# Feed-forward as block products: w_out decoded during the attention, y's operands in the experts' slots, wo's loads at group 26, five operand buffers in turn

## The chip, the cores and the metric

One NeuronCore of a Trainium2 chip runs the program. The metric is the device time of one execution in microseconds (us), the median of the runs shown. TensorE is called PE here, VectorE DVE, ScalarE ACT, GpSimd POOL and SyncE SP. SP issues all of this kernel's transfers, one after the other; DVE, ACT, PE, POOL and SP each work through their own list in order, and wait for each other by semaphores.

## What is computed

Three steps stand one behind the other; all arrays are float32 in the reference.

```python
def phi(x):                       # attention with 128 random features, 4 batches x 8 heads x 576 x 64
    h = np.einsum('bhsd,md->bhsm', x, omega) - np.sum(x * x, axis=-1, keepdims=True) / 2.0
    return np.exp(h - np.max(h, axis=-1, keepdims=True)) / np.sqrt(m)
kv = np.einsum('bhsm,bhsd->bhmd', k_p, v)
num = np.einsum('bhsm,bhmd->bhsd', q_p, kv)      # divided by q_p . sum of k_p: x, 2304 tokens x 512

for e in range(E):                # 8 experts, each token goes to the one with the largest logit
    he = np.maximum(x[mask] @ w1[e], 0.0)        # 512 -> 1024 -> 512
    out[mask] = gate_w[mask, None] * (he @ w2[e])

h = x @ w_in                      # the feed-forward: 512 -> 2048 -> 512 for all 2304 tokens
g = h * (1.0 / (1.0 + np.exp(-1.702 * h)))
return (g @ w_out).astype(np.float32)
```

## The kernel before

**Precision.** Every product is made of three matmuls. An operand x is split in two: hi is x rounded by an ACT copy to the type fp32r, lo is x - hi by a subtraction (on DVE, for some weights on POOL); hi x hi, hi x lo and lo x hi are added up in PSUM. Wherever a split is named below, it is one ACT instruction and one subtraction behind it (line 785).

**Attention and experts, merged.** The attention (a generator, line 741) and the experts (`moe_gen`, line 660) run merged by a ratio of work until the attention ends; then the experts go on alone. An expert pass b takes the 576 tokens of batch b in two halves of 288; a half does 8 products xh, xl x w into h1h, h1l (12 matmuls each) and then the second layer into the y tiles, which go to `y_dram`. Weights come through staging tiles st and are split into the slots wh0 to wh7 and wl0 to wl7 of the pool `moe`, which also holds xh, xl, h1h, h1l and y.

**The feed-forward as block products.** Both factors use a scheme with 7 products where a 2 x 2 block product has 8; the operands are sums and differences of blocks, made by `mix` (four additions into the last places of a tile z). The raw weights arrive as 64-bit words and are decoded by DVE with three integer operations per tile `raw` (`decode`, line 758).
- `prep_in(j)` (line 805): two raws of w_in, decode, mix on POOL, split into wih, wil (pool `ring`, two of each).
- `prep_out(j)` (line 821): two raws of w_out, decode, mix on POOL, two stores into `wo_dram` (768 and 128 KB). Eight of them, j = 0 to 7.
- `prep_y(b)` (line 838): two halves kp of the features of batch b; loads of z from `y_dram`, mix (POOL for kp 0, DVE for kp 1), split into yc.
- `first(j, b)` (line 974): 32 groups, the "quads", of 7 products x 6 matmuls of 128x288; ACT and DVE take the sums out of PSUM (s1, u2, u3, h), ACT applies the gate function, and two stores go to `g_dram`.
- `second(k)` (line 1072): 9 blocks of 256 tokens, 7 products x 24 matmuls of 128x256; the left operands are sums of quarters of gt, split into gs; the right ones are wo, loaded from `wo_dram` and split (`prep_w`, line 1040).

**What sets the order.** The list `jobs` holds the prep generators; `work()` advances the first of them by one step each time it is called, once per step of the experts or of a group. Before the change the list gets six `prep_out` when the attention ends (line 927), and w_in 0 and 1, y0 and the last two `prep_out` when all but one of the experts are through (line 936); y1 to y3 are put in only after the experts (line 948), when the pool `moe` has been given up for `rp`. The program's final order on each engine then comes from the compiler's scheduler.

**Buffers.** z has two buffers, raw three, gs three slots in turn: one tile of `l2` and two tags of `ring` (line 1083, two buffers each). gt (line 1052) is one tile of 256 tokens, loaded by two transfers with runs of 512 B, so a tile is free again when its last reader is through.

## Time and profile before

| what | value |
|---|---|
| median of 3 runs | 838.25 us (834.89 to 841.78) |
| the profiled execution | 839.54 us, its span 837.7 us |
| mean granted clock of TensorE in it | 0.959 |
| PE busy | 763.2 us (91%), 5922 matmuls |
| DVE busy | 517.7 us (62%) |
| ACT busy | 353.6 us (42%) |
| POOL busy | 204.8 us (24%) |
| moved by DMA | 126.64 MB, mean 151 GB/s |

The span runs from the first to the last instruction of the profiled execution. Busy time is the time in which an engine has an instruction under way; PE's matmuls are pipelined, so a busy PE can still do fewer matmuls than it could, and the count beside the busy time says how many. The attention ends at about 320 us, the experts at about 420, the first factor at about 625 with its last groups, and the second runs to the end. "A <- B" in a list of waits means that A stood still until B had ended.

### The profile page before, as it was taken

What the parts mean: (1) busy time and instruction counts of PE and PEld (TensorE: products, weight loads), DVE (VectorE), ACT (ScalarE), POOL (GpSimd) and SP (SyncE); (2) the same over time, 40 slices, a digit from 0 to 9 for tenths busy, and PEclk for the clock granted to TensorE, in tenths of its full rate; (3) what the DMA queues carried; (4) which work ended last, traced back from release to release, by engine and by line L of the source; (5) the groups of instructions that cost most, each with busy time, mean ns of one, the idle gap of its engine ahead of it and who ended that gap; (6) DMA issues with size and microseconds to landing.
All of it is one profiled execution on the core that took longest, in us unless ns stands there. A gap on an engine that the chain in (4) does not pass through costs nothing.

```text
span 837.7 us, 15256 instructions
## 1 busy us (share of the span) xinstructions
PE 763.2 (91%) x5922; PEld 735.0 (88%) x5922; DVE 517.7 (62%) x1130; ACT 353.6 (42%) x687; POOL 204.8 (24%) x158
## 2 busy tenths in 40 slices
PE   7997999999999998999747999999964999899996
PEld 6876999989999997999737999999964999899896
DVE  5877675768752625986826754423475676567653
ACT  5554653445233323223324655555663333333231
POOL 3455495165004400454332431100000000000000
PEclk9999899999999999999967999999995999999999
DMA  5556945467223306996572653344593545554411
GB/s 157 132 143 137 280 109 154 110 195 157 54 82 109 99 27 193 326 321 216 173 226 87 221 193 139 115 150 164 179 355 102 127 126 126 126 127 126 126 26 29
DMA packets 158319, 126.64 MB, mean 151 GB/s; under 512 B 63904, under 2 KB 139680, under 8 KB 157344
## 3 DMA queue, kind: packets, MB, share of 16 engines
q1 hardware_dynamic: 158240, 125.59, 51.1%
q8 instruction: 48, 0.79, 0.4%
q14 instruction: 31, 0.25, 0.1%
HBM read 78.69 MB, written 40.39 MB: 142 GB/s over the span
## 4 chain that ended last, share of the span: by engine, by line
PE 62%; DMA 14%; DVE 11%; ACT 4%; issue 3%; POOL 3%; SPq 2%; POOLq 0%; ACTq 0%; DVEq 0%
PE m_ps L110 18%; PE pa L983 10%; DMA gt<-g_dram 6%; PE qa L1095 5%; PE pc L983 5%; PE qm L1095 4%; PE w_ps L110 3%; DVE gs L787 3%; PE num L414 3%; PE pb L983 3%; PE kv_ps L372 2%; PE pb L1095 2%; DMA z<-wo_dram 2%; PE tq L400 1%; PE pr L314 1%
## 5 line engine op out<-in xcount | busy, mean ns | idle before, releaser
L983 PE MATMUL pa<-yc,wih 128*128 128x288 f32 x512 | 112.3, 307 | 19.8 <-ACT yc L786 12.7
L983 PEld LDWEIGHTS pa<-yc,wih 128*128 128x128 f32 x512 | 86.4, 196 | 23.3 <-ACT yc L786 14.1
L110 PE MATMUL m_ps<-xh,wh 128*128 128x288 f32 x256 | 78.9, 308 | 4.9 <-DVE h1l L678 4.9
L1095 PE MATMUL qa<-wo,gs 128*128 128x256 f32 x648 | 82.6, 283 | 0.4 <-ACT gs L786 0.4
L1095 PEld LDWEIGHTS qa<-wo,gs 128*128 128x128 f32 x648 | 79.7, 190 | 1.0 <-ACT gs L786 0.9
L645 POOL TENSOR_TENSOR wl<-st,wh 128x1024 fp32r<-128x1024 f32 x23 | 54.5, 2375 | 94.8 <-ACT wh L643 94.7
L983 PE MATMUL pa<-yc,wil 128*128 128x288 f32 x256 | 77.5, 303 | 0.0
L110 PE MATMUL m_ps<-xh,wl 128*128 128x288 f32 x256 | 76.6, 299 | 0.0
L110 PE MATMUL m_ps<-xl,wh 128*128 128x288 f32 x256 | 76.5, 299 | 0.0
L999 DVE TENSOR_TENSOR h<-pc,u 128x288 f32<-128x288 f32 x64 | 28.1, 454 | 68.4 <-PE pc L983 55.3
L786 ACT ACTIVATE gs<-gt 128x1024 fp32r<-128x1024 f32 x36 | 38.1, 1059 | 71.8 <-PE qm L1095 45.7
L783 POOL TENSOR_TENSOR z<-z 128x256 f32<-128x256 f32 (+1 forms) x48 | 43.2, 920 | 99.4 <-DVE z L767 78.2
L1095 PE MATMUL qm<-wo,gs 128*128 128x256 f32 x432 | 58.8, 292 | 8.6 <-DVE gs L787 7.5
L1095 PEld LDWEIGHTS qm<-wo,gs 128*128 128x128 f32 x432 | 55.6, 198 | 10.3 <-DVE gs L787 8.7
L329 DVE TENSOR_REDUCE small<-pr 128x4 f32<-128x512 f32 (+1 forms) x80 | 51.1, 639 | 13.7 <-PE pr L321 6.3
L678 DVE SCALAR_TENSOR_TENSOR h1l<-m_ps,h1h 128x288 fp32r<-128x288 f32 x64 | 28.9, 453 | 46.4 <-ACT h1h L675 46.2
L643 ACT ACTIVATE wh<-st 128x1024 fp32r<-128x1024 f32 (+1 forms) x33 | 33.9, 1033 | 54.3 <-DMA st<-in_moe_w_dram 23.9
L1000 ACT ACTIVATE g<-h 128x288 f32<-128x288 f32 x96 | 40.2, 439 | 36.2 <-DVE h L999 31.4
L787 DVE TENSOR_TENSOR gs<-gt,gs 128x1024 fp32r<-128x1024 f32 x36 | 44.0, 1222 | 18.1 <-ACT gs L786 18.0
L983 PE MATMUL pc<-yc,wih 128*128 128x288 f32 x256 | 54.4, 297 | 0.1
L110 PEld LDWEIGHTS m_ps<-xh,wh 128*128 128x128 f32 x256 | 48.7, 190 | 5.9 <-DVE h1l L678 5.3
L675 ACT ACTIVATE h1h<-m_ps 128x288 fp32r<-128x288 f32 x64 | 25.7, 405 | 59.1 <-PE m_ps L110 58.8
(175 smaller groups left out, 2039.3 us busy)
## 6 DMA issues: line engine op xcount, KB each, us to landing
g_dram<-g SPq DMA_DIRECT2D x64, 288.0 KB, 2.5
gt<-g_dram SPq DMA_DIRECT2D x16, 1024.0 KB, 9.0
st<-in_moe_w_dram SPq DMA_DIRECT2D x31, 512.0 KB, 5.3
raw<-in_moe_w_out_dram SPq DMA_DIRECT2D x16, 512.0 KB, 6.0
raw<-in_moe_w_in_dram SPq DMA_DIRECT2D x16, 512.0 KB, 4.9
z<-wo_dram SPq DMA_DIRECT2D x7, 1024.0 KB, 6.7
wo_dram<-z SPq DMA_DIRECT2D x8, 768.0 KB, 5.3
y_dram<-y SPq DMA_DIRECT2D x32, 144.0 KB, 3.6
```

The lines of the kernel that those rows point to most:

```text
L110: ins = nc.tensor.matmul(out=ps, lhsT=a, rhs=b, start=start and n == 0, stop=stop and n == 2)
L329: nc.vector.tensor_reduce(out=pm, in_=ps[:, :w], axis=AX.X, op=ALU.max, negate=on_act)
L643: nc.scalar.activation(out=hi[:, :, s], in_=st[:, :, s], func=ACTF.Copy)
L645: eng.tensor_tensor(out=lo[:, :, s], in0=st[:, :, s], in1=f32(hi)[:, :, s], op=ALU.subtract)
L678: nc.vector.scalar_tensor_tensor(out=hl[:, f], in0=ps, scalar=0.0, in1=f32(hh[:, f]), op0=ALU.max, op1=ALU.subtract)
L783: eng.tensor_tensor(out=z[:, o], in0=z[:, a], in1=z[:, b], op=op)
L786: nc.scalar.activation(out=hi, in_=src, func=ACTF.Copy)
L787: eng.tensor_tensor(out=lo, in0=src, in1=f32(hi), op=ALU.subtract)
L983: nc.tensor.matmul(out=ps, lhsT=w[:, a, kp], rhs=x[:, kp, y], start=start and kp + m == 0, stop=kp == 1 and m == 2, skip_group_check=True,)
L999: nc.vector.tensor_tensor(out=h, in0=ps, in1=add, op=ALU.add)
L1000: nc.scalar.activation(out=dst, in_=h, func=ACTF.Gelu_apprx_sigmoid)
L1095: nc.tensor.matmul(out=ps, lhsT=x[:, f], rhs=w[i][:, f], start=start and f + m == 0, stop=f == NP - 1 and m == 2, skip_group_check=True,)
```

## The change

It touches five things.
1. **w_out's eight jobs** run in a pool `early` of their own, from the 200th step of the merged loop on, one step of a job every third step. The pool has one z and two raw buffers, and before each raw load ACT writes one element of the raw tile from the last h1h result (`mark`), so that the load can't start ahead of that expert's work.
2. **y's operands** get homes in slots that are there already: y0 in the pool `r0`, made as soon as the attention ends; y1 in w0 to w3, y2 in xh, xl, w4 and w5, made during the last expert when the slots are given up (`chunks`); y3 in w6, w7, h1h and h1l, made after it. The halves hi and lo of a weight become one tile w0 to w7 for it. The pools `rp` and `l2` go.
3. **The order of the last eight groups** is by b, and wo's loads come by the table `after`: wo0 and gt 0 behind group 25 (the 26th), wo1 and wo2 behind group 27, wo3 and wo4 behind 29, the last two behind the first step of block 0.
4. **gt** is loaded in two tiles, one for each half of the features, with runs of 1 KB.
5. **The operands gs** take five places in turn (two tags of `ring` and the two z buffers, and one tile of `l1`) where there were three.

```diff
+    EARLY = 200
+    early = tc.alloc_tile_pool(name="early", bufs=1, side="right")
...
-        hi = moe.tile(shape, F32R, tag=f"wh{c}", name=f"wh{c}")
-        lo = moe.tile(shape, F32R, tag=f"wl{c}", name=f"wl{c}")
+        w = moe.tile([P, 2] + shape[1:], F32R, tag=f"w{c}", name=f"w{c}")
+        hi, lo = w[:, 0], w[:, 1]
...
                 nc.scalar.activation(out=hh[:, f], in_=ps, func=ACTF.Relu)
+                mark[0] = f32(hh[0:1, f, 0:1])
...
-        raw = pool.tile([P, DM], I64, tag="raw", name="raw", bufs=3)
+        raw = pool.tile([P, DM], I64, tag="raw", name="raw", bufs=2)
+        if pool is early:
+            nc.scalar.activation(out=raw.bitcast(F32)[0:1, 0:1], in_=mark[0], func=ACTF.Copy)
...
-        return pool.tile(shape, F32, tag="z", name="z", bufs=2)
+        return pool.tile(shape, F32, tag="z", name="z", bufs=1 if pool is early else 2)
...
+    def prep_y(zpool, b, homes, chunks):
         for kp in range(2):
+            while prep["free"] < 2 * NW * (B - 1) + chunks[kp]:
+                yield "wait"
+            hi, lo = (slot(*homes[2 * kp + i], [P, 7, HS], f"y{'hl'[i]}") for i in range(2))
...
+        early_jobs = [prep_out(early, j) for j in range(NP)]
...
             tick()
+            if clock[0] >= EARLY and clock[0] % 3 == 0:
+                work(early_jobs)
         att_done[0] = True
...
-        r0 = None
-        jobs += [prep_out(fw, j) for j in range(6)]
+        r0 = tc.alloc_tile_pool(name="r0", bufs=1)
+        homes = [[(r0, f"r{i}") for i in range(4)]]
+        homes += [[(moe, f"w{i}") for i in range(4)]]
+        homes += [[(moe, "xh"), (moe, "xl"), (moe, "w4"), (moe, "w5")]]
+        homes += [[(moe, "w6"), (moe, "w7"), (moe, "h1h"), (moe, "h1l")]]
+        jobs.append(prep_y(fw, 0, homes[0], (0, 0)))
...
-                jobs += [prep_in(fw, ring, 0), prep_in(fw, ring, 1), prep_y(fw, 0, y0), prep_out(fw, 6), prep_out(fw, 7)]
-            work()
+                jobs += [prep_in(fw, ring, 0), prep_in(fw, ring, 1)]
+                jobs += [prep_y(fw, 1, homes[1], (NW, NW)), prep_y(fw, 2, homes[2], (NW, NW + 2))]
+            work(early_jobs)
+            work(jobs, 2 if x_done[0] == B else 1)
...
-        quads += [(6, 0), (6, 1), (7, 0), (7, 1), (6, 2), (7, 2), (6, 3), (7, 3)]
+        quads += [(j, b) for b in range(B) for j in (NP - 2, NP - 1)]
...
+            parts = [pool.tile([P, NP, 2 * P], F32, tag=tg, name="gt", bufs=1) for pool, tg in g_homes[k % 2]]
...
+        GS = ((ring, "wh", 2), (ring, "wl", 2), (fw, "z", 2), (fw, "z", 2), (l1, "gs", 1))
...
-                pool, tg, n = ((l2, "gs", 1), (ring, "wh", 2), (ring, "wl", 2))[operands[0] % 3]
+                pool, tg, n = (l1, "gs", 1)
+                if operands[0]:
+                    pool, tg, n = GS[(operands[0] - 1) % len(GS)]
...
+        after = {
+            25: [lambda: prep_w(0), lambda: gts.update({0: load_g(0)})],
+            27: [lambda: prep_w(1), lambda: prep_w(2)],
+            29: [lambda: prep_w(3), lambda: prep_w(4)],
+        }
...
-            if n == 28:
-                prep_w(0)
-                gts[0] = load_g(0)
-                prep_w(1)
-            if n in (29, 30, 31):
-                prep_w(n - 27)
```

In the rows below, a number behind a name tells tiles of one name apart, and what stands in brackets is what the instruction waits for.

**DVE just behind the attention's last step (the copy tot_i).** Before, the decode of the first w_out job (z<-raw) stands there, between two h1l splits of the expert pass b = 2.

```order
L678 SCALAR_TENSOR_TENSOR h1l_4364<-m_ps_4409,h1h_4363 128x288 [waits Activation_49]
L911 CAST tot_i_3906<-small_116 128x1 [waits PE_49]
L760 TENSOR_SCALAR z_3946<-raw_3928 128x512 [waits DMAHW4_49,DMAHW5_49,DMAHW3_49,DMAHW6_49,SP_sequencer_49,DVE_49]
L764 SCALAR_TENSOR_TENSOR z_3946<-raw_3928,z_3946 128x512 [waits DVE_49]
L760 TENSOR_SCALAR z_3946<-raw_3930 128x512 [waits DMAHW7_49]
L767 SCALAR_TENSOR_TENSOR z_3946<-raw_3928,z_3946 128x512 [waits DVE_49]
L764 SCALAR_TENSOR_TENSOR z_3946<-raw_3930,z_3946 128x512 [waits DVE_49]
L645 TENSOR_TENSOR wl1_4442<-st_4161,wh1_4441 128x1024 [waits DMAHW5_49,PE_49,Activation_49]
L678 SCALAR_TENSOR_TENSOR h1l_4364<-m_ps_4426,h1h_4363 128x288 [waits Activation_49]
L760 TENSOR_SCALAR z_4019<-raw_4001 128x512 [waits DMAHW0_49]
```

After, two more h1l splits are done ahead of the block, and the place is taken by the mix of y0's second half (z_4239<-z_4239), the two lo halves of y0 (yl), two operations of w_in's decode (z_4607) and a weight split:

```order
L651 TENSOR_TENSOR w1_4495<-st_4267,w1_4495 128x1024 [waits DMAHW5_49,PE_49,Activation_49]
L686 SCALAR_TENSOR_TENSOR h1l_4425<-m_ps_4498,h1h_4424 128x288 [waits Activation_49]
L791 TENSOR_TENSOR z_4239<-z_4239 128x288 [waits DMAHW2_49,DMAHW3_49,DMAHW1_49,DMAHW4_49,SP_sequencer_49,DVE_49]
L941 CAST tot_i_4034<-small_119 128x1 [waits PE_49]
L791 TENSOR_TENSOR z_4239<-z_4239 128x288 [waits DMAHW3_49]
L791 TENSOR_TENSOR z_4239<-z_4239 128x288 [waits DVE_49] x2
L795 TENSOR_TENSOR yl_4168<-z_4169,yh_4167 128x2016 [waits DMAHW7_49,DMAHW0_49,Activation_49]
L795 TENSOR_TENSOR yl_4238<-z_4239,yh_4237 128x2016 [waits Activation_49]
L768 TENSOR_SCALAR z_4607<-raw_4587 128x512 [waits DMAHW6_49,DMAHW5_49,DVE_49]
L768 TENSOR_SCALAR z_4607<-raw_4589 128x512 [waits DMAHW6_49]
L651 TENSOR_TENSOR w2_4530<-st_4478,w2_4530 128x1024 [waits DMAHW4_49,Activation_49]
L686 SCALAR_TENSOR_TENSOR h1l_4425<-m_ps_4515,h1h_4424 128x288 [waits Activation_49]
```

The decode of w_out has left the place; the h1l split that follows now stands behind y0's whole chain.

**ACT where the experts end and the first groups begin.** Before, the splits of y1, y2 and y3 (yc2, yc4, yc6) stand among the evacuations of the first groups (s1, u2 from PSUM, g through the gate function):

```order
L1000 ACTIVATE g_5309<-h_5390 128x288 [waits DVE_49]
L786 ACTIVATE yc2_5231<-z_5248 128x2016 [waits DMAHW4_49,DMAHW3_49,Pool_49]
L786 ACTIVATE yc2_5231<-z_5276 128x2016 [waits DMAHW5_49,DMAHW4_49,DVE_49]
L786 ACTIVATE yc4_5233<-z_5304 128x2016 [waits DMAHW0_49,DMAHW7_49,Activation_49,Pool_49]
L990 ACTIVATE s1_5406<-pa_5399 128x288 [waits PE_49,Activation_49]
L990 ACTIVATE s1_5494<-pa_5487 128x288 [waits PE_49,Activation_49]
L1000 ACTIVATE g_5397<-h_5417 128x288 [waits DVE_49]
L1000 ACTIVATE g_5308<-h_5452 128x288 [waits DVE_49]
L990 ACTIVATE u2_5442<-pa_5399 128x288 [waits PE_49]
L786 ACTIVATE yc4_5233<-z_5343 128x2016 [waits DMAHW3_49,DMAHW2_49,DVE_49]
```

After, only y3 (yh_5272) stands behind the experts' last h1h (h1h_5019); y2's second half (yh_4927) comes before the first s1:

```order
L682 ACTIVATE h1h_5019<-m_ps_5130 128x288
L794 ACTIVATE yh_4927<-z_4929 128x2016 [waits DMAHW2_49,DMAHW3_49,DVE_49,PE_49]
L1012 ACTIVATE s1_5270<-pa_5263 128x288 [waits PE_49]
L1012 ACTIVATE s1_5341<-pa_5334 128x288 [waits PE_49]
L1012 ACTIVATE u2_5300<-pa_5263 128x288 [waits PE_49]
L1012 ACTIVATE u2_5378<-pa_5334 128x288 [waits PE_49]
L1022 ACTIVATE g_5261<-h_5285 128x288 [waits DVE_49]
L1012 ACTIVATE s1_5425<-pa_5418 128x288 [waits Activation_49]
L1012 ACTIVATE u3_5327<-pa_5263 128x288 [waits PE_49]
L1012 ACTIVATE u3_5411<-pa_5334 128x288 [waits PE_49]
L794 ACTIVATE yh_5272<-z_5274 128x2016 [waits DMAHW4_49,DMAHW2_49,Pool_49]
L1022 ACTIVATE g_5262<-h_5329 128x288 [waits DVE_49]
```

The splits of y1 and y2 moved ahead, in among the h1h of the last expert.

**ACT where the first factor ends.** Before, the splits of wo5 and wo6 follow the last g, and the operands of the first block (gs) follow them:

```order
L786 ACTIVATE wo4_7433<-z_7431 128x2048 [waits DMAHW2_49]
L1000 ACTIVATE g_7436<-h_7526 128x288 [waits DVE_49]
L786 ACTIVATE wo5_7532<-z_7530 128x2048 [waits DMAHW4_49,PE_49]
L786 ACTIVATE wo6wh_7540<-z_7538 128x2048 [waits DMAHW2_49]
L786 ACTIVATE gs_7603<-gt_7218 128x1024 [waits PE_49,Activation_49]
L786 ACTIVATE gs_7544<-s1_7506 128x1024
```

After, the same two splits, wo6 first, stand ahead of the last g and of the operand gs_7540, which the third product of block 0 reads:

```order
L1022 ACTIVATE g_7431<-pa_7432 128x288 [waits DMAHW1_49,PE_49]
L1022 ACTIVATE g_7431<-h_7492 128x288 [waits DVE_49]
L794 ACTIVATE wo6wh_7536<-z_7534 128x2048 [waits DMAHW5_49,PE_49]
L794 ACTIVATE wo5h1h_7526<-z_7524 128x2048 [waits DMAHW3_49,PE_49]
L1022 ACTIVATE g_7430<-h_7520 128x288 [waits DVE_49]
L794 ACTIVATE gs_7540<-s1_7500 128x1024
L794 ACTIVATE gs_7571<-s1_7500 128x1024 [waits DVE_49,Activation_49]
```

The order between the last wo splits and that operand is the same; two of the earlier wo splits (wo3, wo4) are further ahead than they were.

## Rows read from the trace of the kernel before

**Rows 1.** 40-us windows: busy (count) of PE, PEld, DVE, ACT, POOL; clock; DMA; GB/s.

```profile
200.00:240.00 40.00, 40.00 (x358) 37.92 (x357) 27.20 (x98) 13.33 (x33) 2.38 (x1) 1.00 0.29 70
240.00:280.00 40.00, 40.00 (x329) 39.14 (x328) 17.29 (x58) 13.54 (x24) 10.96 (x5) 1.00 0.37 113
280.00:320.00 40.00, 40.00 (x314) 38.38 (x314) 18.54 (x79) 12.42 (x29) 8.02 (x4) 1.00 0.19 61
...
400.00:440.00 40.00, 23.64 (x136) 21.08 (x134) 21.90 (x34) 12.38 (x18) 16.56 (x16) 0.80 0.64 201
440.00:480.00 40.00, 34.87 (x222) 33.86 (x223) 28.27 (x44) 21.11 (x43) 13.27 (x12) 0.86 0.48 157
480.00:520.00 40.00, 40.00 (x303) 40.00 (x302) 21.25 (x40) 22.07 (x53) 9.56 (x12) 1.00 0.50 170
...
600.00:640.00 40.00, 21.97 (x158) 20.57 (x157) 24.25 (x24) 21.46 (x33) 0.00 (x0) 0.81 0.91 298
```

**Rows 2.** Waits of PE in 300:400: engine, line, releaser: us, times, longest.

```profile
PE m_ps L110 <- DVE h1l L678: 4.9, 2, 4.0
```

**Rows 3.** Chain of waits in 315:346: start, us, what.

```profile
325.25 4.80 DMA raw<-in_moe_w_out_dram
...
330.17 0.44 DVE z L760
...
334.64 0.38 DVE h1l L678
```

**Rows 4.** Waits of PE in 400:480.

```profile
PE pa L983 <- ACT yc L786: 12.7, 5, 6.0
```

**Rows 5.** Chain of waits in 398:456.

```profile
419.00 8.00 DMA wo_dram<-z
...
428.85 3.74 DMA z<-y_dram
...
432.75 4.35 POOL z L783 x3
...
438.00 1.90 ACT yc L786
439.92 2.27 DVE yc L787
```

**Rows 6.** Chain of waits in 590:646.

```profile
629.12 6.67 DMA z<-wo_dram
...
635.81 1.92 ACT wo6wh L786
...
637.75 2.29 DVE wo6wl L787
...
641.24 4.83 PE pb L1095 x22
```

**Rows 7.** Waits of PE in 645:840.

```profile
PE qm L1095 <- DVE gs L787: 7.5, 5, 2.3
```

**Rows 8.** Waits of DVE in 640:838.

```profile
DVE s L1077 <- DMA gt<-g_dram: 20.8, 5, 5.6
```

**Rows 9.** DVE by line in 320:480: shapes, count; busy, mean ns; idle before, releasers.

```profile
L764 DVE SCALAR_TENSOR_TENSOR z<-raw,z 128x512 int32<-128x512 int32 x24 | 19.0, 797 | 0.3
...
L767 DVE SCALAR_TENSOR_TENSOR z<-raw,z 128x512 int32<-128x512 int32 x24 | 17.2, 725 | 0.2
L760 DVE TENSOR_SCALAR z<-raw 128x512 int32<-128x512 int32 x26 | 14.3, 561 | 6.7 <-DMA raw<-in_moe_w_out_dram 4.6 <-DMA wo_dram<-z 1.5 <-DMA raw<-in_moe_w_in_dram 0.3
```

**Rows 10.** POOL by line in 320:480.

```profile
L831 POOL TENSOR_TENSOR z<-z 128x256 f32<-128x256 f32 x32 | 30.5, 973 | 76.0 <-DMA raw<-in_moe_w_out_dram 40.9 <-DVE z L767 32.7 <-ACT g L1000 2.3
```

**Rows 11.** The page's DMA issues: KB each, median us to landing.

```profile
wo_dram<-z SPq DMA_DIRECT2D x8, 768.0 KB, 5.3
```

**Rows 12.** Timeline of DVE: start, us, instruction.

```profile
332.90 1.74 DVE L645 TENSOR_TENSOR wl<-st,wh 128x1024 fp32r<-128x1024 f32 x1
```

**Rows 13.** The page's costliest groups: busy, mean ns; idle before, releaser.

```profile
L787 DVE TENSOR_TENSOR gs<-gt,gs 128x1024 fp32r<-128x1024 f32 x36 | 44.0, 1222 | 18.1 <-ACT gs L786 18.0
```

115 lines of the change are left out of this document (58 added, 57 removed).

## Prediction

> **What bounds the kernel now.** I read the 40-us windows first, because they show where TensorE (PE) runs short. At full rate the first factor of the feed-forward does 303 matmuls in 40 us with the clock at 1.00 [rows 1], so one 128x288 matmul takes 0.132 us. A 128x256 one then takes 0.132 x 256/288 = 0.117 us (an estimate). PE is the bound almost everywhere; what can be won is the places where its count drops. The waits of PE and the chain of waits say what it lacked at each. There are four such places, and the rows give each a price.
> - **A, just after the attention.** PE waits 4.9 us for h1l [rows 2]. The chain shows why: the w_out load was issued at 325.25 and took 4.80, the decode began at 330.17, and the h1l split behind it on DVE came at 334.64 [rows 3].
> - **B, experts to feed-forward.** 400:440 and 440:480 hold 136 + 222 = 358 matmuls where 606 fit, so 248 x 0.132 = 32.7 us are lost [rows 1]. PE waits 12.7 us for ACT's half of the operands yc [rows 4]. The chain is serial: an 8.00 us store of a w_out mix ahead of the y loads on SP, a load of 3.74, three POOL mixes of 4.35, an ACT split of 1.90, a DVE split of 2.27 [rows 5].
> - **C, first to second factor.** 600:640 holds 158 of 303 [rows 1]: 145 x 0.132 = 19.1 us. The chain there is a load, an ACT split and a DVE split of wo6; PE restarts at 641.24, 1.2 us after the window, and its first 22 matmuls take 4.83 instead of 22 x 0.117 = 2.6 [rows 6]. Together 19.1 + 1.2 + 2.2 = 22.5 us.
> - **D, the nine blocks of the second factor.** PE waits 7.5 us, in five pieces, for operand splits on DVE [rows 7], and DVE waits 20.8 us, in five pieces, for gt [rows 8].
>
> **The change part by part.** Base: the profiled execution, 839.5 us, which lies 1.3 above the median of the runs, inside their spread of 6.9.
>
> **E, w_out's decode goes into the attention: +3.** Eight jobs move. Each is two raws of three DVE operations, 2 x (0.561 + 0.797 + 0.725) = 4.17 us [rows 9], so 33.3 us of DVE; four POOL mixes of 0.973 each [rows 10], so 3.9 a job; one store of 5.3 [rows 11]. What hides it: from 200 us on PE is busy 40.00 of 40, while DVE has 12.8 us idle in the tightest of the three windows to 320 and POOL is nearly empty [rows 1]. In three such windows that is at least 38 us against 33.3. The catch is order: the pool early has one z buffer, so each job's first decode stands at DVE's head until the job before has mixed (3.9) and stored (5.3), 9.2 us, and the attention's own DVE work queues behind it. The order puts 14 to 28 DVE instructions between most jobs, which at the 0.38 us of a short one, the h1l split of rows 3, is 5.3 to 10.6 us and roughly covers that. Bounds: nothing, if all is covered; 12, if half of what is left over in the closest pairs reaches PE. I take 3, near the lower end, because PE shows no wait at all in that stretch today.
>
> Beside POOL's mix a DVE split of 1024 columns takes 1.74 us [rows 12], against 1.22 for the same shape in the second factor, when POOL is idle [rows 13]: 0.52 more. If each of the 32 mixes costs DVE that once, 17 us are added to DVE, most of them in its idle time; I leave that inside the 3.
>
> The Trainium skill (SBUF — State Buffer, Who interferes with whom) says that a DVE instruction with two SBUF inputs contends with a GpSimd instruction that reads SBUF, and that the later one blocks until the first is finished. The trace agrees in direction: 1.74 against 1.22. By the row the 32 mixes add 17 us to DVE; by the rule they could add up to 32 x 0.973 = 31, and E would be nearer its upper bound, the sum at about 816. It speaks against moving POOL and decode work beside a busy DVE.
>
> **A, y0 in place of the decode: +6.** The decode leaves, but y0's mixes and splits come in. Their loads go out no earlier than the raw loads did (325.25), so by rows 5 the first half is loaded at 329.0, mixed on POOL at 333.3, split on ACT at 335.2 and on DVE at 337.5. The second half, mixed on DVE meanwhile, ends on ACT at 337.1 and on DVE at 337.5 + 2.27 = 339.8. Two decode operations of w_in (2 x 0.56) and a weight split (1.74) stand before the next h1l, which ends at 343.0. Before it ended at 335.0: 8.0 later. But two h1l splits (12 matmuls of PE each, 3.2 us) now come before the block: 8.0 - 3.2 = +4.8. A second place, the first w_in split that PE wants while the last expert starts, adds about 1 by its DVE length; sum +6. Bounds: 0, if y0's chain lies beside work that PE still has; 13, if PE stands still for both places.
>
> **B, y's operands in the experts' slots: -27.** y0, y1 and y2 are made during the last expert, so the first groups start with their operands there. Only y3 is made after it: store and load (each about 3.74), mix 4.35, ACT 1.90, DVE 2.27, so 16.0 us after the experts' end. PE has about 30 us of other groups to do (228 matmuls stand in its order between the experts' last and the first that reads y3), but ACT's order puts y3's split, which waits for POOL until 11.8, ahead of the evacuations that free PSUM. Eight evacuations stand before it, some 8 x 6 x 0.132 = 6.3 us of PE; 11.8 + 1.9 - 6.3 = 7.4 are open, of which the three banks that PE may still fill cover 2.4. So 5 us remain: 32.7 - 5 = 27.7; I take 27. Bounds 21 (the whole of 7.4 and DVE's two splits are on the path) and 31 (only a short restart).
>
> **C, wo's loads from group 26 on: -7.** The two weights that end last are still wo5 and wo6, because z has two buffers and their loads wait for the DVE splits of wo3 and wo4. From the end of group 29: the loads of wo3 and wo4 together land at about 8 and 9 (a single one took 6.67 [rows 6]); ACT splits (1.92) end at 9.9 and 11.8, DVE splits (2.29) at 12.2 and 14.5; the loads of wo5 and wo6 land at 18.9 and 21.2; ACT splits wo6 and wo5 until 25.0, DVE until 27.7, and the operand of the third product comes behind both, at 28.9. PE meanwhile has groups 30 and 31, 84 x 0.132 = 11.1, and two products, 48 x 0.117 = 5.6: 16.7. It stands 12.2, and restarts slowly, 2.2: 14.4 against 22.5, a gain of 8. The g stores and gt loads share the queue, so I take 7. Bounds: 0, if each load needs as long beside them as the 8.00 of the store in rows 5, and the first pair twice that; 20, if they land while the groups run.
>
> **D, gt in two parts and five operand buffers: -7.5.** The first part of a gt is free one product earlier and its rows are twice as long; with five buffers DVE can work four products (some 11 us) ahead, so a gt that lands late no longer reaches PE. I take the whole wait of rows 7. Bounds 3 (only the waits at block starts go) and 11 (the slower clock behind the waits goes too).
>
> Sum: 839.5 + 3 + 6 - 27 - 7 - 7.5 = 807.0. The runs lie 1.3 lower: **806**.
>
> **The rivals.**
> - **C is hidden altogether** (chance 0.17). If the transfers take 6.67 even in pairs and ACT reaches the operand before wo5, PE stands only a few microseconds: about 10 less, 796. For it: 600:640 had its DMA load because everything came at once. Against: ACT's order, which puts wo6 and wo5 first.
> - **A and E eat more** (0.14). At their upper bounds, 13 + 12 instead of 9, it is 822; with B at its lower bound, 828. For it: DVE and ACT are in order and A already is a head-of-line wait [rows 3].
> - **The change doesn't do what it says** (0.04): if y1 to y3 wait for slots that the last expert holds to its end, B stays as it is: 806 + 24 = 830 to 838.
> - **Slower** (0.05). The 9.2 us between jobs of E is not covered: 8 x 9.2 = 74 us of DVE standing in the attention, with the 17 of POOL's mixes on top at worst. From 33 / 8 = 4.1 us per job that reach PE the gain is gone; at 9.2 it is about 877. For it: one z buffer, and the mark that ties a raw load to the expert's progress. Against: PE has no wait there now, with DVE at 27.20 of 40.
>
> **How the numbers follow.** The forecast has the other 0.60 and by itself 795 to 818. The range 790 to 828 holds it, the first rival and most of the second; outside lie the last two and the tails, under 0.2. About 1% is what a measurement of this kernel can tell from no change. Faster by over 1% (under 830): forecast, first and second rival less a little, 0.88; within 1%: 0.07; slower: 0.05.
>
> **What would show it.** E: PE still 40.00 of 40 in 200:320, no DVE wait for an earlier job's store there over 5 us. A: a PE wait for h1l of 8 to 13 us between 325 and 350. B: no wo_dram store and one y chain after the experts' end; matmuls in the 80 us from there at over 550. C: a single PE wait for gs of 8 to 14 us. D: PE's waits in the blocks under 2 us in sum. I am wrong if PE falls short in 200:320, or if B keeps more than 10 us.

## The result

The changed kernel takes 813.86 us, the median of four runs (812.01 to 816.57), against 837.36 for the kernel before; the ratio is 0.9716 with a 95% interval of 0.9663 to 0.977. That is faster, inside the range that was forecast and 8 us above the forecast. A second set of four runs, beside the experiments, gave 812.93 (ratio 0.9719, 0.9675 to 0.9763). The profiled execution took 812.29 us with a span of 810.3.

A sum can only be compared stage by stage if the stages are cut at the same place in the program. I cut both traces where the same matmul ends: at the attention's last matmul, at the experts' last, at the 336th and the 1176th of the first factor (of 1344), and at the 168th of the second (of 1512). The windows between these cuts, first of the kernel before (columns as in [rows 1]; a matmul that crosses a cut is counted on both sides):

```profile
0.00:324.80 324.80, 310.62 (x2535) 290.22 (x2535) 206.77 (x713) 143.60 (x331) 131.11 (x78) 0.98 0.49 130
324.80:402.50 77.70, 72.83 (x534) 72.23 (x533) 61.27 (x96) 20.33 (x31) 31.15 (x36) 0.98 0.83 273
402.50:480.10 77.60, 56.11 (x339) 52.54 (x338) 47.77 (x72) 33.59 (x61) 29.83 (x28) 0.82 0.57 181
480.10:591.80 111.70, 111.70 (x843) 111.70 (x842) 45.85 (x87) 60.61 (x146) 12.74 (x16) 1.00 0.41 146
591.80:657.30 65.50, 46.70 (x339) 45.00 (x338) 39.96 (x39) 33.12 (x50) 0.00 (x0) 0.84 0.69 216
657.30:838.00 180.70, 165.27 (x1345) 163.31 (x1343) 116.05 (x127) 62.38 (x70) 0.00 (x0) 0.98 0.41 103
```

and of the changed kernel:

```profile
0.00:342.50 342.50, 319.91 (x2571) 298.18 (x2571) 232.01 (x763) 146.13 (x348) 154.62 (x110) 0.98 0.61 170
342.50:424.60 82.10, 72.71 (x517) 70.98 (x516) 47.37 (x65) 26.85 (x34) 18.00 (x20) 0.94 0.44 136
424.60:469.40 44.80, 43.49 (x322) 42.44 (x321) 30.09 (x52) 25.78 (x57) 10.04 (x12) 1.00 0.51 170
469.40:581.80 112.40, 111.47 (x842) 111.24 (x841) 47.23 (x87) 62.08 (x146) 12.45 (x16) 1.00 0.42 148
581.80:640.70 58.90, 47.71 (x338) 46.50 (x337) 39.69 (x42) 33.26 (x51) 0.00 (x0) 0.88 0.76 261
640.70:811.00 170.30, 161.64 (x1345) 161.23 (x1344) 113.06 (x125) 60.30 (x69) 0.00 (x0) 0.99 0.36 103
```

At full rate a 128x288 matmul takes 0.1325 us (111.70 us for 843 of them in the fourth window of the kernel before, with the clock at 1.00), and a stage's loss is its length less that for each of its matmuls. In the first stage the merge puts 36 more expert matmuls (4.8 us) in front of the attention's end, which is taken off. So:

| stage | forecast | before | changed | difference |
|---|---|---|---|---|
| E, to the attention's end, at the same work | +3 | 324.8 | 342.5 - 4.8 | +12.9 |
| A, to the experts' end, lost | +6 | 6.9 | 13.6 | +6.7 |
| B, to the 336th matmul of the first factor, lost | -27 | 32.7 | 2.1 | -30.6 |
| the groups between | 0 | 111.7 | 112.4 | +0.7 |
| C, to the 168th matmul of the second factor | -7 | 65.5 | 58.9 | -6.6 |
| D, to the end of the span | -7.5 | 180.4 | 169.6 | -10.8 |
| sum | -32.5 | | | -27.7 |

The spans differ by 27.4. Four terms came within 1 us of the forecast or were 3 to 4 us better; one, E, cost 10 more.

**E in the rows.** The 40-us windows of the changed kernel that answer to [rows 1]:

```profile
200.00:240.00 40.00, 36.94 (x313) 34.65 (x311) 30.50 (x78) 13.21 (x34) 11.12 (x11) 0.96 0.67 200
240.00:280.00 40.00, 38.36 (x306) 36.97 (x305) 24.98 (x86) 13.62 (x34) 17.56 (x15) 1.00 0.79 251
280.00:320.00 40.00, 35.64 (x264) 33.98 (x263) 24.95 (x66) 11.40 (x24) 18.42 (x16) 0.91 0.53 169
```

From 200 to 320 us, where PE had 40.00 of 40 in every window, it now has 36.94, 38.36 and 35.64, and the granted clock is 0.96 and 0.91 in two of them. DVE's busy time there rose only by 17 us in sum, to 30.50, 24.98 and 24.95: by its mean it still looks idle for about a quarter of the time or more. The decode took what was forecast, 16 instructions of each form, together 32.0 us against 33.3 (DVE by line, 200 to 342 us; columns as in [rows 9]):

```profile
L775 DVE SCALAR_TENSOR_TENSOR z<-raw,z 128x512 int32<-128x512 int32 x16 | 13.7, 862 | 0.0
...
L772 DVE SCALAR_TENSOR_TENSOR z<-raw,z 128x512 int32<-128x512 int32 x16 | 11.5, 729 | 0.0
...
L768 DVE TENSOR_SCALAR z<-raw 128x512 int32<-128x512 int32 x16 | 6.8, 450 | 13.4 <-DMA raw<-in_moe_w_out_dram 6.8 <-DMA wo_dram<-z 4.4 <-issue 2.2
```

The last row also holds the waits that were feared: 13.4 us in which DVE stood at the head of its line for a raw load (6.8), an earlier job's store (4.4) or nothing the profile shows (2.2).

From 200 us to the attention's end PE was never idle before. Now it is idle for 142.50 - 133.44 = 9.1 us:

```profile
200.00:342.50 142.50, 133.44 (x1046) 126.96 (x1043) 89.79 (x276) 46.05 (x109) 47.10 (x42) 0.96 0.61 189
```

The granted clock of 0.96 adds to that. It fell from 2.4 to 1.2 GHz twice there: at 212.8, behind two idle pieces of PE of 1.5 and 0.8 us, and at 294.7, inside the longest idle piece of 3.6 us. By (1 - 0.96) x 142.5 it cost some 5 to 6 us more at most (an estimate). The longest of PE's waits is not for DVE but for ACT's qpT, and its chain can be followed back (PE's waits, 200 to 342 us; ACT's timeline):

```profile
PE tq L402 <- ACT qpT L404: 3.6, 1, 3.6
```

```profile
282.20 0.20 ACT L800 ACTIVATE raw<-h1h 1x1 f32<-1x1 f32 x1 [6.04 <-DVE z L775]
...
294.36 1.06 ACT L649 ACTIVATE w<-st 128x1024 fp32r<-128x1024 f32 x1 [4.12 <-DMA st<-in_moe_w_dram]
```

The qpT stands on ACT behind a weight split, for whose load ACT waited 4.12 us. SP issued that load at 288.89, as soon as one of POOL's two weight splits (286.48 to 291.19) had freed its tile. These came late because their ACT halves stood behind two marks, for which ACT had waited 6.04 and 1.93 us for DVE's decode, and because POOL was still mixing an early job until 286.52. f1_changed, further down, repeats this with 3.0 us of PE. In all, 4.3 us of PE's waits there name ACT and 3.8 DVE.

Before, DVE's idle time in this stretch was made of short waits, most of them for ACT (200 to 325 us; total, times, longest):

```profile
DVE h1l L678 <- ACT h1h L675: 29.7, 18, 4.5
```

**A in the rows.** PE's waits between 335 and 430 us, answering to [rows 2]:

```profile
PE m_ps L110 <- DVE h1l L686: 5.1, 4, 2.5
PE w_ps L110 <- ACT h1h L682: 3.8, 1, 3.8
```

and the chain (columns as in [rows 3]), over y0's ACT split, y0's DVE splits, and two decode operations to a weight split, behind which h1l ends and PE goes on at 357.96:

```profile
349.38 1.89 ACT yh L794
351.30 1.83 DVE yl L795
...
355.64 0.76 DVE z L768 x2
356.40 1.13 DVE w L651
```

The profile puts ACT's wait before y0's split down to a weight load, but by its own record that load landed only at 350.47. POOL's mix of y0 ended at 349.35, 0.03 us before the split began (POOL's timeline):

```profile
346.07 3.28 POOL L791 TENSOR_TENSOR z<-z 128x288 f32<-128x288 f32 x3 [0.63 <-DMA z<-y_dram]
```

PE was idle for 77.70 - 72.83 = 4.9 us in this stage before and for 82.10 - 72.71 = 9.4 us now, and the granted clock fell from 0.98 to 0.94.

**C and D in the rows.** The chain at the end of the first factor, answering to [rows 6]:

```profile
602.30 1.93 ACT wo3xh L794
...
609.48 2.28 DVE gs L795 x2
...
611.80 4.04 PE qm L1119 x19
...
616.54 1.92 ACT wo6wh L794
...
622.98 1.15 DVE gs L795
...
624.17 5.36 PE qa L1119 x24
```

PE waits twice: until 611.80 for the operands that stand behind wo4's split, and until 624.17 for the one that stands behind wo6's and wo5's. In the blocks, PE's waits for operands, 7.5 us in [rows 7], are gone; what is left there is

```profile
PE qm L1119 <- DVE u L1133: 1.8, 1, 1.8
```

### The profile page after: what moved, and what is told of

It reads as the page before. It is cut to its first block, busy times and chain, and to the rows that moved or that the text cites. A ratio compares the mean times of both kernels' runs of the same rounds, so it can differ in the third digit from the quotient of the medians.

```text
span 810.3 us, 15293 instructions
## 1 busy us (share of the span) xinstructions
PE 756.9 (93%) x5922; PEld 730.6 (90%) x5922; DVE 509.4 (63%) x1130; ACT 354.4 (44%) x703; POOL 195.1 (24%) x158
## 4 chain that ended last, share of the span: by engine, by line
PE 68%; DMA 11%; DVE 10%; issue 4%; ACT 3%; SPq 2%; POOL 2%; DVEq 0%; ACTq 0%; POOLq 0%
PE m_ps L110 14%; PE qa L1119 12%; PE pa L1005 10%; PE qm L1119 6%; PE pc L1005 5%; DMA st<-in_moe_w_dram 4%; PE w_ps L110 3%; PE pb L1119 3%; PE pb L1005 3%; PE num L416 3%; PE kv_ps L374 2%; DMA m<-in_k_dram 2%; DMA raw<-in_moe_w_out_dram 1%; PE pr L316 1%; PE tq L402 1%
## 5 line engine op out<-in xcount | busy, mean ns | idle before, releaser
L110 PE MATMUL m_ps<-xh,w 128*128 128x288 f32 x512 | 118.2, 308 | 5.9 <-DVE h1l L686 5.9
L110 PEld LDWEIGHTS m_ps<-xh,w 128*128 128x128 f32 x512 | 87.9, 194 | 7.6 <-DVE h1l L686 7.2
L110 PE MATMUL m_ps<-xl,w 128*128 128x288 f32 x256 | 77.9, 304 | 0.0
L1005 PE MATMUL pa<-yh,wih 128*128 128x288 f32 x256 | 75.6, 296 | 2.2 <-ACT u L1012 1.3
L1005 PE MATMUL pa<-yl,wih 128*128 128x288 f32 x256 | 75.4, 295 | 0.0
L1005 PE MATMUL pa<-yh,wil 128*128 128x288 f32 x256 | 75.0, 295 | 0.0
L110 PE MATMUL m_ps<-h1h,w 128*128 128x288 f32 x320 | 70.8, 301 | 1.2 <-DVE h1l L686 0.7
L651 POOL TENSOR_TENSOR w<-st,w 128x1024 fp32r<-128x1024 f32 x23 | 55.0, 2398 | 35.8 <-ACT w L649 34.7
L110 PEld LDWEIGHTS m_ps<-h1h,w 128*128 128x128 f32 x320 | 52.8, 188 | 1.9 <-DVE h1l L686 0.8
L795 DVE TENSOR_TENSOR gs<-gt,gs 128x1024 fp32r<-128x1024 f32 x36 | 43.7, 1220 | 13.5 <-ACT gs L794 13.4
L110 PEld LDWEIGHTS m_ps<-xl,w 128*128 128x128 f32 x256 | 49.8, 195 | 0.2
```

The lines of the kernel that those rows point to most:

```text
L110: ins = nc.tensor.matmul(out=ps, lhsT=a, rhs=b, start=start and n == 0, stop=stop and n == 2)
L651: eng.tensor_tensor(out=lo[:, :, s], in0=st[:, :, s], in1=f32(hi)[:, :, s], op=ALU.subtract)
L795: eng.tensor_tensor(out=lo, in0=src, in1=f32(hi), op=ALU.subtract)
L1005: nc.tensor.matmul(out=ps, lhsT=w[:, a, kp], rhs=x[:, y], start=start and kp + m == 0, stop=kp == 1 and m == 2, skip_group_check=True,)
```

## The experiments

Each kernel is the changed one with the edit shown. Besides the time, the stage sums of its one profiled execution are given, cut as above: E is the attention's end less 0.1325 us for each expert matmul before it; A, B and "groups" are losses; C and D (here to the last matmul) are lengths. A matmul that crosses a cut is counted once here, so that A and B differ by up to 0.6 from the table above.

| kernel | median us | ratio, 95% interval | E | A | B | groups | C | D |
|---|---|---|---|---|---|---|---|---|
| before | 837 | 1 | 191.6 | 7.3 | 33.1 | 0.3 | 65.5 | 174.4 |
| changed | 813.9 | 0.9663 to 0.9770 | 204.5 | 14.1 | 2.7 | 1.2 | 58.9 | 163.2 |
| f1_changed | 812.9 | 0.9675 to 0.9763 | 204.9 | 14.7 | 1.7 | 1.2 | 59.4 | 162.2 |
| e1_prefetch | 807.5 | 0.9607 to 0.9687 | 207.0 | 10.0 | 1.4 | 1.2 | 59.0 | 161.2 |
| e2_no_mark | 835.9 | 0.9960 to 1.0013 | 233.8 | 11.7 | 2.3 | 1.2 | 59.0 | 161.2 |
| e3_late_out | 807.7 | 0.9610 to 0.9690 | 203.3 | 15.7 | 2.4 | 1.2 | 59.2 | 161.2 |
| e4_y0_late | 811.1 | 0.9651 to 0.9730 | 208.5 | 11.3 | 2.4 | 1.2 | 59.1 | 161.2 |
| f2_pool_store | 808.5 | 0.9612 to 0.9699 | 209.6 | 8.1 | 2.4 | 1.2 | 58.3 | 161.2 |
| f3_one_op | 802.1 | 0.9537 to 0.9626 | 197.5 | 14.2 | 2.2 | 1.2 | 58.5 | 161.2 |
| f4_gs3 | 812.4 | 0.9643 to 0.9739 | 206.8 | 14.5 | 1.3 | 1.2 | 57.2 | 163.8 |
| g1_gt_rows | 812.6 | 0.9687 to 0.9750 | 201.7 | 13.5 | 1.8 | 1.2 | 59.7 | 161.2 |
| g2_y_after | 814.5 | 0.9673 to 0.9779 | 207.1 | 14.1 | 1.8 | 1.2 | 59.5 | 162.9 |
| g3_groups_op5 | 801.2 | 0.9538 to 0.9603 | 192.7 | 15.3 | 1.2 | 9.1 | 55.3 | 161.2 |
| h1_y_tied | 832.0 | 0.9918 to 0.9984 | 200.7 | 13.3 | 16.5 | 1.2 | 57.1 | 173.1 |

How far these sums can be read: six of the traces (changed, f1, f4, g1, g2, h1) run the same attention, and their E lies between 200.7 and 207.1, their A between 13.3 and 14.7, the sum of both between 214.0 and 221.4. A single E that differs by 3 says nothing.

### What E costs

**e1_prefetch**, the next job's raws loaded two steps sooner:

```diff
         for o, a, b, op in ((4, 1, 0, ALU.subtract), ...):
             nc.gpsimd.tensor_tensor(out=z[:, o], in0=z[:, a], in1=z[:, b], op=op)
+        if j + 1 < NP:
+            ahead[j + 1] = [load_raw(pool, 1, f) for f in (j + 1, j + 1 + NP)]
         yield
```

> Each early job's two raw loads go out in the step that mixes the job before, two steps sooner; work, buffers and marks stay. The changed kernel runs at 813.9 us and PE is 13 us behind at the attention's end. Theory E1, DVE stands in line for a raw load or for the last job's store (6.8 + 4.4 us of its waits between 200 and 342 us): the raw part goes, 807 to 810. Theory E2, the moved work itself (32 us of DVE, 23 of POOL, 14 MB) is what slows the attention: no change, 812 to 816.

It took 807.5 us. But the reason is not the one expected: DVE's wait for the raw load fell from 6.8 to 2.3 us, while its wait in the same place for the earlier job's store grew from 4.4 to 10.6, with another 6.5 of no shown cause (DVE's waits, 200 to 342 us; total, times, longest):

```profile
DVE z L768 <- DMA wo_dram<-z: 10.6, 4, 4.2
...
DVE z L768 <- issue: 6.5, 1, 6.5
...
DVE z L768 <- DMA raw<-in_moe_w_out_dram: 2.3, 1, 2.3
```

So the line at DVE's head got longer, and neither E (207.0 against 204.5 and 204.9) nor the sum of E and A (217.0 against 218.6 and 219.6) moved beyond its spread. The time is 5 to 6 us lower than the changed kernel's, with intervals that overlap; where those 5 us lie the one profile does not show. Theory E1 as it was put, a DVE wait that turns into PE's, is not borne out.

**e2_no_mark**, without the copies that tie the loads to the experts:

```diff
-        if pool is early:
-            nc.scalar.activation(out=raw.bitcast(F32)[0:1, 0:1], in_=mark[0], func=ACTF.Copy)
```

> The one-element ACT copies ahead of the early raw loads are left out; nothing else that is computed changes. ACT waited 13.9 us for DVE's decode in four of these copies. Theory E3, ACT's place in line (the copies hold back qpT and h1h behind them) is the cost: 806 to 809. Theory E1, DVE's line: the same wait only moves to SP, 812 to 815; and if the loads then come too early and meet the attention's own, 815 to 820.

835.9 us, against every theory: the scheduler pulled the jobs forward into the attention's first 200 us (the issues of their stores lie between 21.7 and 201.8), and E rose by 29. At 200 us PE had done 875 of the attention's matmuls and 253 of the experts', where the changed kernel had done 1120 and 409. So the run does not say what ACT's waits for the marks cost. What it shows is that the same decode costs more in the first 200 us, where the changed kernel's DVE is busy for 26 to 30 us of 40 and its POOL for 18 to 26. (The changed kernel has no early job there; from 200 to 320 us, before, DVE was busy for 17 to 27 us of 40 and POOL for under 11 [rows 1].) That fits E2, but it does not exclude the others.

**e3_late_out**, the jobs handed out behind the attention:

```diff
-    EARLY = 200
+    EARLY = 100000
```

> The early jobs are handed out only after the attention's last step; the scheduler can still pull them ahead as far as the marks let it, into the last fifth of the attention. Theory E1: PE is at most 8 us behind at the attention's end, and the rest comes back between there and the last expert, where the jobs now meet y0 and w_in: 810 to 825 in all. Theory E2: the sum of the loss in both stretches stays 13 + 7 us, 812 to 816.

807.7 us, but with stage sums like the changed kernel's: E 203.3, A 15.7. The marks allowed the scheduler to put the decode of six of the eight jobs into the attention's last part all the same, so this edit did not separate the theories; the sum of E and A, 219.0, is the 218.6 and 219.6 of the changed kernel, as E2 says.

**f1_changed** is the changed kernel again.

> The changed kernel itself once more, beside the next three. 812 to 815 if its distance to e1 (807.5) and e3 (807.7) is theirs; 807 to 810 if it is the chip's day. In its trace PE is 20 us later than before by the experts' end, counted at the same number of matmuls.

812.9, as the changed kernel had. Its interval overlaps those of e1 and e3 by a little, so that it is not settled whether these two are faster; their stage sums don't show where they would be.

**f2_pool_store**, the early stores on POOL's queue:

```diff
-        nc.sync.dma_start(out=wo_dram[0, :, j], in_=z[:, 0])
-        nc.sync.dma_start(out=wo_dram[1:7, :, j].rearrange("o p d -> p o d"), in_=z[:, 2:8])
+        nc.gpsimd.dma_start(out=wo_dram[0, :, j], in_=z[:, 0])
+        nc.gpsimd.dma_start(out=wo_dram[1:7, :, j].rearrange("o p d -> p o d"), in_=z[:, 2:8])
```

> The early jobs' two stores go out from POOL's queue, right behind the mixes, instead of SP's. In the changed kernel SP waits 22.3 us for DVE and 13.8 for POOL at these stores, between 200 and 342 us, with weight loads and y stores queued behind. Theory E4, SP's line delays the experts' weights (ACT waits 12.6 us for st) and so PE: the loss by the experts' end falls from 20 to about 12 us, 804 to 807. Theory E1 or E2: no change against the changed kernel of this call; the POOL queue's own cost per store could make it 2 to 4 slower.

808.5 us. SP's waits at the stores, in f1_changed (200 to 342 us)

```profile
SPq L843 <- DVE z L775: 20.4, 4, 6.7
SPq L844 <- POOL z L841: 12.9, 7, 5.0
...
SPq L807 <- ACT raw L800: 7.6, 6, 2.1
```

are gone, but a part of them moved to the next thing in SP's line, the raw loads, in f2_pool_store:

```profile
SPq L807 <- ACT raw L800: 27.9, 8, 10.0
```

The experts' weights came sooner (ACT's wait for st fell from 12.5 to 7.7 us), and the sum of E and A is 217.7, inside the spread. The time is 4 us better and the intervals overlap. Some of the loss may lie in SP's line; it is not the most of it.

**f3_one_op**, two of the three decode operations on w_out left out:

```diff
+        if short:
+            return
         nc.vector.scalar_tensor_tensor(
             out=w, in0=r[:, :, 1], scalar=-0x40000000, in1=w, op0=ALU.bitwise_and, op1=ALU.bitwise_or
```

> Leaves out two of the three decode operations on w_out (its values are then not those of the reference): 6.8 us of DVE stay of 32; raw loads, mixes, stores, marks and buffers stay. Theory E2, DVE's extra work is what the attention can't hide: the loss by the experts' end falls from 20 to 10 us or less, 801 to 804. Theory E1 or E4, the lines at DVE's and SP's heads: at most 3 us better.

802.1 us, 10.8 below f1_changed, with intervals that don't meet (0.9537 to 0.9626 against 0.9675 to 0.9763). E falls to 197.5, the only one of these that is below the spread. From 200 us to the attention's end PE is idle for 131.00 - 125.85 = 5.2 us instead of 9.1, and the granted clock is 0.99 instead of 0.96:

```profile
200.00:331.00 131.00, 125.85 (x1009) 120.06 (x1008) 68.75 (x241) 44.58 (x108) 46.94 (x42) 0.99 0.63 201
```

The loads, stores, marks, mixes and the single z buffer are all still there. DVE's waits at the head of its line even grew, from 13.4 to 16.3 us, so the gain does not lie in E1's line. The operation that stayed took 9.5 us instead of 6.8. So the larger part of E hangs on the decode's work on DVE, as E2 says: 25 us of operations were taken away and 11 us of time came back, 7 of them in E (204.9 to 197.5). By which way this work reaches PE the run does not show, because what others wait for the decode shrank with it: ACT at the marks from 15.0 to 8.1 us, SP at the first store from 20.4 to 13.4. About 6 us of E (197.5 against 191.6) stay with the rest.

### What stands in A

**e4_y0_late**, y0 made with y1 and y2:

```diff
-        jobs.append(prep_y(fw, 0, homes[0], (0, 0)))
...
-                jobs += [prep_in(fw, ring, 0), prep_in(fw, ring, 1)]
+                jobs += [prep_in(fw, ring, 0), prep_in(fw, ring, 1), prep_y(fw, 0, homes[0], (0, 0))]
```

> y0's operands are made at the start of the last expert, beside y1 and y2, and not as soon as the attention ends; w_in 0 then takes its place behind the attention. Theory A1, the two y0 splits (4.4 us of DVE, 3.7 of ACT) are what h1l waits for: the loss between the attention's and the experts' end falls from 14 to 7 us, 807 to 810. Theory A2, the loads that wait for the attention's release are the cost, whatever stands there: 812 to 815. If the last expert has no room for a third y, the first groups wait and it is 815 to 820.

811.1 us, within the spread of the changed kernel's. A falls by 3 (11.3), E is 4 higher, and the sum is the same, 219.8. w_in 0's decode took y0's place behind the attention. A2 is the better account: the place stands for loads that go out after the attention's release, whether they feed y0 or w_in; y0's own splits are at most 3 of the 7 us. The last expert had room for a third y: B stayed at 2.4.

### What B's gain is made of

**g2_y_after** raised the thresholds at which y1 and y2 may be made:

```diff
-                jobs += [prep_y(fw, 1, homes[1], (NW, NW)), prep_y(fw, 2, homes[2], (NW, NW + 2))]
+                jobs += [prep_y(fw, 1, homes[1], (NW + 4, NW + 4)), prep_y(fw, 2, homes[2], (NW + 4, NW + 4))]
```

> y1 and y2 wait for the last expert's end as y3 does; homes, y0 and w_out's early decode stay. Lost between the experts' end and the 336th matmul of the first factor: 33.1 us before, 2.7 in the changed kernel. Theory B1, having y1 and y2 ready is the gain: 15 to 25 us are lost there, 826 to 836. Theory B2, it is enough that w_out's stores and decode are out of the way: under 10, 815 to 820.

814.5 us and B 1.8: nothing changed, because the order of instructions came out as it was. The thresholds don't hold y back at these values; what does (the slots, most likely) the run does not show. It decides nothing about B, and serves as a third measurement of the changed kernel.

**h1_y_tied** ties them to the last expert's last y, and undoes two edits of D together:

```diff
+            if b in (1, 2):
+                nc.scalar.activation(out=z[0:1, 0, 0:1], in_=last_y[0], func=ACTF.Copy)
+                nc.scalar.activation(out=z[0:1, 1, 0:1], in_=last_y[0], func=ACTF.Copy)
+                nc.scalar.activation(out=z[0:1, 2, 0:1], in_=last_y[0], func=ACTF.Copy)
...
+                pool, tg, n = ((l1, "gs", 1), (ring, "wh", 2), (ring, "wl", 2))[operands[0] % 3]
...
+            parts = [pool.tile([P, NF2, P], F32, tag=tg, name="gt", bufs=1) for pool, tg in g_homes[k % 2]]
```

> Two edits in stages that don't touch. First, y1's and y2's loads can't start before the last expert's last y is written (a one-element ACT copy into z ties them to it); homes, y0 and the early decode of w_out stay. Theory B1, having y1 and y2 early is the gain: 15 to 25 us lost between the experts' end and the 336th matmul of the first factor, where the changed kernel loses 1.7 and before lost 33.1. Theory B2, it is enough that w_out's stores and decode are away: under 8. Second, the operands have three places and gt is cut by tokens (each alone left the blocks at 161 to 164 us; before took 174). Theory D2c, either one suffices and both gone lose it: 170 to 176. Theory D3, it is the two separate gt tiles that remain: 160 to 166. In all 824 to 850 under B1, 813 to 820 under B2 with D3.

832.0 us. B loses 16.5 us, where the changed kernel loses 1.7 to 2.7 and before lost 33.1. The chain of y1 now shows behind the experts' end as it did in [rows 5], load, POOL mix, ACT split, DVE split, PE:

```profile
421.28 3.58 DMA z<-y_dram
...
425.76 1.78 POOL z L793 x2
427.57 1.90 ACT yh L796
429.49 2.27 DVE yl L797
```

So B's 31 us have two parts: about 14 (16.5 - 2.2) come from having y1 and y2 early, B1. The other 17 (33.1 - 16.5) are with what h1 leaves in place, above all that the decode and stores of w_out are elsewhere, B2; before, the y loads stood behind them (the 8.00 us store in [rows 5]). No run takes this second part alone.

### What D's gain is made of

**f4_gs3** has three operand places again, gt in its new parts:

```diff
-                pool, tg, n = (l1, "gs", 1)
-                if operands[0]:
-                    pool, tg, n = GS[(operands[0] - 1) % len(GS)]
+                pool, tg, n = ((l1, "gs", 1), (ring, "wh", 2), (ring, "wl", 2))[operands[0] % 3]
```

> The operands gs have three places in turn again (one of l1, two tags of ring), gt stays in two parts. Theory D1, the five places made the gain of 11 us in the second factor: the blocks take 172 to 175 us again from the 168th matmul to the last, and the time rises by 8 to 11. Theory D2, the gt parts made it: no more than 2 us slower.

812.4 us, D 163.8: the five places alone are not the gain. DVE's wait for gt, 20.8 us in [rows 8], is small with the new parts:

```profile
DVE s L1099 <- DMA gt<-g_dram: 5.7, 6, 3.6
```

**g1_gt_rows** has the five places, but gt cut by tokens, with the short runs of before:

```diff
-            parts = [pool.tile([P, NP, 2 * P], F32, tag=tg, name="gt", bufs=1) for pool, tg in g_homes[k % 2]]
+            parts = [pool.tile([P, NF2, P], F32, tag=tg, name="gt", bufs=1) for pool, tg in g_homes[k % 2]]
...
-                        in_=g_dram[b][h * NP:(h + 1) * NP, :, q0:q0 + m].rearrange("f p n -> p f n"),
+                        out=t[:, :, o:o + m], in_=g_dram[b][:, :, q0:q0 + m].rearrange("f p n -> p f n")
```

> gt stays in two tiles, but cut by tokens (128 x all 16 feature blocks, runs of 512 B) and not by feature halves (runs of 1 KB); the five places stay. The changed kernel takes 812.9 us, its blocks 162 from the 168th matmul to the last. Theory D2a, the cut by halves (half 0 free early, longer runs) made D's gain: the blocks take 168 to 175, time 818 to 825. Theory D2b, any cut with five places does: within 2 us.

812.6 us, D 161.2. Here DVE waits as long for gt as it ever did,

```profile
DVE s L1098 <- DMA gt<-g_dram: 21.1, 7, 4.1
```

and PE does not notice: with five places DVE is far enough ahead. With both undone, in h1_y_tied, the blocks take 173.1 us again, the kernel before's 174.4 nearly, and both waits are back:

```profile
PE qm L1122 <- DVE gs L797: 7.1, 4, 2.5
```

```profile
DVE s L1104 <- DMA gt<-g_dram: 16.2, 4, 4.8
```

So either edit alone gives the whole gain, one by making gt arrive in time, the other by hiding that it doesn't.

### A version that beats both

**g3_groups_op5** moves w_out's jobs into the first factor's groups, where DVE was the least busy, and splits block 0's third operand before wo5 and wo6:

```diff
-        early_jobs = [prep_out(early, j) for j in range(NP)]
...
+        OUT_AT = (7, 8, 10, 12, 14, 16, 18, 20)
         for n, (j, b) in enumerate(quads):
...
+            if n in OUT_AT:
+                jobs.append(prep_out(fw, OUT_AT.index(n)))
...
             ops[7] = halves_of(a21)
-            yield
             ops[5] = halves_of(s1)
+            yield
```

> w_out's eight jobs go neither into the attention nor into the experts but into the first factor's groups 7 to 20, from pool fw, where DVE is busy 16 to 21 of 40 us and POOL under 9; and block 0's third operand is split before wo5 and wo6. Theory E2 (DVE's work is too much for the attention): the loss of 13 us there goes, and the groups lose under 4; theory C1 (the operand behind wo6 and wo5 on ACT and DVE is C's wait): C shrinks by 3 to 6 us, together 793 to 800. If the groups can't hide it (DVE standing for raw loads ahead of h), they lose 10 or more: 806 to 815. If C's wait is wo5 itself, 798 to 803.

801.2 us, ratio 0.9538 to 0.9603, 12 us below the changed kernel, with intervals that don't meet. That is above the 793 to 800 which E2 and C1 together were expected to give. E is 192.7, nearly that of before, and PE is idle for 0.15 us from 200 us to the attention's end: the attention's cost is gone with w_out's jobs. That fits f3, though here the loads, mixes and stores are gone with the decode. C is 55.3, 3.6 to 4.1 below the changed kernel's and 1.8 below the lowest of the others (57.1), which is C1's share. But the groups are no free place either: they lose 9.1 us instead of 1.2. PE waits for DVE's h and ACT's u (480 to 640 us):

```profile
PE pc L998 <- DVE h L1014: 4.3, 5, 1.7
...
PE pa L998 <- ACT u L1005: 2.3, 4, 1.1
```

So w_out's jobs cost PE 8 us there against 12 to 13 in the attention.

## Why the prediction came out as it did

- **The total.** It lies 8 us above the forecast. The terms make 5 of these (-27.7 instead of -32.5): E cost 10 more, and B and D gave 7 of it back by being better than forecast, which is luck. The other 3 are the step from a profiled execution to the median: the runs before lay 1.3 below their profiled execution, and the changed kernel's lie 1.6 above theirs.
- **B, -27 forecast, -30.6 measured.** Right in mechanism and within 4 us, at the upper of the bounds that were set. PE's idle time gives 20 of it (21.5 to 1.3 us), the clock, 0.82 before and 1.00 now, the rest. y3's chain, priced at 5 us of PE, cost 3 at most. h1 shows that having y1 and y2 early is a little under half of it.
- **A, +6 forecast, +6.7 measured.** The chain is the one that was written out: y0's load and POOL's mix (8.8 us from 340.54 to 349.35, forecast as 8.1), y0's ACT split, both DVE splits (4.43 us were forecast as 4.54), two decode operations, a weight split, h1l. But the forecast sign, 8 to 13 us of PE waiting for h1l, did not come: it was 5.1 us in four pieces, and 3.8 for h1h. PE's idle time grew by 4.5 us, and the lower clock, which the prediction did not price here, added up to 3, so that the near hit is in part luck. The prediction put the cause on y0's chain; e4 shows that w_in 0's decode, loaded after the attention's release too, stands there in its stead, so y0 is at most 3 of the 7.
- **C, -7 forecast, -6.6 measured.** PE stood for the third product's operand behind wo6 and wo5, as was forecast from ACT's order; putting it first gave back 2 to 4 us in g3. But it was not the single wait of 8 to 14 us that was forecast: there were two stops, and the first, behind wo4's split, was not in the sum.
- **D, -7.5 forecast, -10.8 measured.** The waits went as forecast. PE's idle time fell by more than these waits, from 15.4 to 8.7 us, and the clock rose from 0.98 to 0.99. The step credited the gt parts and the five places together; the runs show that one would do.
- **E, +3 forecast, +12.9 measured, beyond its bound of 12.** This is the term that was mis-sized. The step that failed: 33 us of DVE work were set against 38 us of idle time in three windows, and only the wait at DVE's head was priced. The size of the work was right (32.0 us). What was wrong is that idle time in a window counts as cover. PE, 40.00 of 40 before, fell short in all three windows, which the prediction itself had named as the sign of being wrong. Before, DVE's idle time there was made of short waits for ACT and PE, and an operation of 0.45 to 0.86 us put between them can delay what follows; other engines wait for the decode too. For PE's longest wait the way is shown above, from the decode over ACT's marks, POOL and a weight load. For the rest it is argued and not shown. Of 25 us of DVE work taken away in f3, 11 came back as time. The wait that was feared did come, 13.4 us of it, but e1 changed it without changing E beyond its spread, and in f3 it grew while E fell. No store of an earlier job held DVE for over 5 us (the longest took 2.6), as was forecast.
- **The rivals.** "Slower" needed 4.1 us per job; measured are 12.9 / 8 = 1.6. "A and E eat more" is the rival that partly came true: 20 us of its 25. C was not hidden altogether. The change did what it says: y1 and y2 stand in the experts' slots. (The 24 us that the rival against this added to 806 should have been B's whole 27.)
- **The rule on the shared port** was weighed at 17 to 31 us of DVE time, nearly all in idle time. In the changed kernel the decode's operations are not longer than in [rows 9] on the whole (0.45, 0.73 and 0.86 us against 0.56, 0.80 and 0.73). DVE's other work did not grow either: 89.8 - 32.0 = 57.8 us from 200 to the attention's end, against 64.2 before. So that is not where E's 13 us lie.

What stays open: the way by which most of the decode reaches PE in E, the 6 us of E that remain in f3, and the 4 to 6 us by which e1, e3 and f2 are below the changed kernel, which their single profiles don't place.

## What to carry to other kernels

A window's idle share is no cover for in-order engines that wait for each other all the time: ask for each piece of moved work whether it can stand in a chain that PE waits on, and expect a part of its length as time (here 11 of 25 us) even where the engine is busy for little more than half the time. Cut two traces at the same matmul, not at the same microsecond; then each term of a sum has its own measurement, and one profile of a kernel with edits in two stages tests both, as far as the spread between traces of the same kernel allows (6 us in E here). When two edits remove the same wait by different means, undoing one of them shows nothing.
